# Who issues the loads of V: from SyncE in two bursts to ScalarE, one piece at a time

## The chip, the cores and the metric

The kernel runs on one core of a Trainium2 chip. The metric is the device time of one execution in microseconds; where a median is given, it is over several executions. The core's engines are named as in the profile: PE (TensorE, matrix products), ACT (ScalarE), DVE (VectorE), POOL (GpSimd) and SP (SyncE, which computes nothing and issues transfers). Each engine works through its own list of instructions in order and waits on semaphores for the others. Transfers (DMAs) can be issued by SP, ACT or POOL.

## What is computed

Causal attention with a decay bias, for 8 batches of 8 heads, 576 positions and 64 dimensions, followed by a gated feed-forward block (SwiGLU) over the 4608 tokens:

```python
scores = scale * q @ k.T
cum = cumsum(max(s, 0))
bias = -(cum[:, None] - cum[None, :])
scores = where(causal, -1e9, scores + min(bias, 0))
attn = softmax(scores)
x = (attn @ v) as [4608 tokens, 512]
g = x @ w_gate                       # 512 -> 1536
out = (g * sigmoid(g) * (x @ w_val)) @ w_out
```

## The kernel before, in words

**Units of work.** The 64 heads (batch times head) are taken in 16 groups of four; the variable `h` counts the groups, `step` the head within a group (0 to 3), and two groups make a batch. The scores of a head are made in four pieces, `ci` 0 to 3 (`score_piece`): PE multiplies K and Q into a PSUM bank (L373), ACT takes the exp into the tile `pt` (L383), POOL clears what lies above the diagonal. Later PE multiplies `pt` with V, which lies in `vt` as bf16 (L410), and DVE normalises the result into `ot` (L427). The feed-forward block works on 512 tokens at a time: PE makes gate and value products (L643), ACT a tanh (L664, tile `th`), DVE two products (L666 `pp`, L677 `ht`), and then PE the down products (L700 for the first two token tiles, L749 for the others), which ACT and DVE copy out (L717, L798, L864).

**Order.** Nothing is left to a scheduler: the generator `attn_items` yields after each small piece of attention, and a loop over the feed-forward items pumps it, so that attention of later heads runs between the feed-forward products of earlier tokens. Each engine's list has the order in which the code records the instructions. PSUM has eight banks, which both halves take and give back in turn.

**Side work.** `side(h, step, ci)` is called after each score piece and records what has to be ready later: the loads of Q and K (`load_qk`, L145), their casts to bf16 on ACT (L258), from group 5 on a way through scratch memory (`scratch`, L274, tiles `ks` and `qs`) and back by a transposing transfer (`transposes`, L284, into `pk` and `pq`), after which DVE copies them into place (`split`, L288, tile `kq`). Attention output of batches 2 and up goes to memory (L444, `xs`, issued by POOL) and comes back by a transposing transfer into `XT` (L451). All transposing transfers, the loads of Q and K, the scratch writes and, in the kernel before, the loads of V are on SP's list, in that order of recording.

**V.** `load_v(b, cs)` (L156) loads pieces of a batch's V as float32 into `rawv`; there are five pieces, 0 to 4, of 128 positions each and 64 for the last, and each piece is one transfer (L162; 256 KB, the last 128 KB, in runs of 256 bytes). `rawv` has one buffer, so the first piece of a batch waits until the batch before has been cast. `side_v` casts the pieces into `vt` (`cast_v`): for batch 2 on POOL, for batches 3 to 7 on ACT (L171), in the odd group before the batch begins. The loads of batch `bn` are recorded in group `h = 2 * bn - 2`: pieces 0 and 1 after head 2's score piece 1, and pieces 2, 3 and 4 after head 3's score piece 1. Pieces 0 and 1 thus stand between the scratch writes of a group's K and Q and the transposing transfers that fetch them, and pieces 2 to 4 behind these.

**Semaphores of transfers.** The tile framework gives each transfer of SP or ACT one of eight completion semaphores and lets it wait, before it is issued, until the transfer that last used this semaphore has landed. The wait stands in the list of the engine that issues.

Of the kernel before, what the change touches and what calls it, by code (L numbers as in the profile page):

```python
# [19 lines left out]
def kernel(  # L20
# [11 lines left out]
    nc = tc.nc  # L32
    PSUM = bass.MemoryType.PSUM

    B, H, S, D = q.shape
# [78 lines left out]
    with tc.manual_schedule():  # L114
# [37 lines left out]
        def load_qk(hb):  # L152
            load_one(hb, "k")
            load_one(hb, "q")

        def load_v(b, cs, eng=nc.sync):  # L156
            if 0 in cs:
                loaded["v", b] = raw.tile([128, NCH, H, D], FP32, tag="rawv", bufs=1, name="rawv")
            t = loaded["v", b]
            for c in cs:  # L160
                n = 128 if c < 4 else TAIL
                eng.dma_start(  # L162
                    t[0:n, c, :, :],
                    v[b, :, c * 128 : c * 128 + n, :].rearrange("h p d -> p h d"),
                )

        def cast_v(b, c, eng):
            n = 128 if c < 4 else TAIL
            dst, src_t = VT[b % 2][0:n, c, :, 0:D], loaded["v", b][0:n, c, :, :]
            if eng is nc.scalar:  # L170
                nc.scalar.copy(dst, src_t)  # L171
            else:
                eng.tensor_copy(dst, src_t)  # L173
# [9 lines left out]
        def aug(hb, engs, hhs=range(HB)):  # L183
            for hh in hhs:
                r, e = divmod(hh, 2)
                r0 = 64 * (1 - r)
                bh = hb * HB + hh
                engs[hh].dma_start(  # L188
                    KQ[hb % 2][r][r0 : r0 + 4, :, e * S : (e + 1) * S],
                    HL[bh : bh + 1, :, :, :],  # L190
                )
# [61 lines left out]
        def cast_one(hb, name, eng):  # L253
            cts[name, hb] = cp.tile([128, J, NR, D], BF16, tag="c" + name, bufs=2, name="c" + name)
            dst = cts[name, hb].rearrange("x j r d -> x r j d")
            src_t = loaded[name, hb]
            if eng is nc.scalar:
                nc.scalar.copy(dst, src_t)  # L258
            else:
                eng.tensor_copy(dst, src_t)  # L260
# [11 lines left out]
        def scratch(hb):  # L272
            for name, SC in (("k", KS), ("q", QS)):
                nc.sync.dma_start(  # L274
                    SC[hb].rearrange("(x j) c -> x (j c)", j=J),
                    cts[name, hb].rearrange("x j r d -> x (j r d)"),
                )
# [3 lines left out]
        def transposes(hb):  # L281
            for name, SC in (("k", KS), ("q", QS)):
                prs[name, hb] = cp.tile([128, NR * S], BF16, tag="p" + name, bufs=1, name="p" + name)
                nc.sync.dma_start_transpose(prs[name, hb], SC[hb])  # L284
# [186 lines left out]
        def do_later(n):  # L471
            while n > 0 and later:
                f, *args = later.pop(0)
                f(*args)
                n -= 1
# [5 lines left out]
        def side(h, step, ci):  # L481
            bh = HB * h + step
            for c in V1_AT.get((bh, ci), ()):
                cast_v(1, c, nc.gpsimd)
            if bh == H + 4 and ci == 3:
                load_v(2, range(5))
            if h == 4 and (step, ci) in ((0, 1), (2, 1)):
                load_qk(6 + step // 2)
            if h >= 5 and h + 3 < NHB and (step, ci) == (0, 1):
                load_qk(h + 3)  # L490
            hb = h + 1
            if NPE <= hb < NHB:
                late = hb == NPE
                if late and (step, ci) == (0, 1):
                    scratch(hb)
                if late and (step, ci) == (0, 3):
                    transposes(hb)
                if (step, ci) == (0, 1):
                    aug(hb, GP4)
                first = 1 if hb < NPE + 3 else 0  # L500
                if step in (first, first + 1) and ci == (3 if late else 1):
                    for r in range(NR):
                        later.append((split, hb, "kq"[step - first], r))
            hb = h + 2
            if hb == NPE and step == 3 and ci % 2 == 1:
                cast_one(hb, "kq"[ci // 2], nc.gpsimd)
            if NPE < hb < NHB:
                six = hb == NPE + 1
                if (step, ci) == ((2, 0) if six else (0, 2)):
                    cast_one(hb, "k", nc.scalar)  # L510
                if (step, ci) == ((2, 2) if six else (1, 2)):
                    cast_one(hb, "q", nc.scalar)
                if (step, ci) == ((3, 0) if six else (2, 0)):
                    scratch(hb)
                if (step, ci) == (3, 3 if six else 0):
                    do_later(NR * 2)
                    transposes(hb)
            if ci != 1:
                return
            bn = h // 2 + 1  # L520
            if 3 <= bn < B:
                if h % 2 == 0:
                    if step == 2:
                        load_v(bn, (0, 1))
                    if step == 3:
                        load_v(bn, (2, 3, 4))

        V2_AT = {(1, 0): 0, (1, 1): 1, (1, 2): 2, (1, 3): 3, (2, 0): 4}
        V_AT = {(1, 0): 0, (2, 0): 1, (2, 2): 2, (3, 0): 3, (3, 2): 4}
# [31 lines left out]
        def attn_items():  # L561
            for kk in range(H, BH + 2):
                h, step = divmod(kk, HB)
                if kk < BH:
                    if step == 0:
                        do_later(NR * 2)
                    if step == 1 and 3 < h + 1 < NPE:
                        cast_one(h + 1, "k", nc.gpsimd)
                        cast_one(h + 1, "q", nc.gpsimd)
                    if step == 2 and 3 < h + 1 < NPE:  # L570
                        aug(h + 1, GP4)
                    for ci in range(4):
                        score_piece(kk, ci)
                        side(h, step, ci)
                        side_v(h, step, ci)
                        yield kk + 0.1 + ci / 8
                        if (step, ci) in PREP_AT.get(h, ()):
                            prep_one(
                                h + 1, PREP_AT[h][step, ci],
                                (nc.scalar, nc.vector)[ci // 2] if h == 2 else None,  # L580
                            )
                            yield kk + 0.1 + ci / 8
# [327 lines left out]
        def pick(side):  # L910
            b = PICK[side]
            for lo in range(2):
                for c0, c1 in ((0, 512), (512, S)):
                    nc.tensor.matmul(
                        banks[:, b + c0 // 512, 0 : c1 - c0], sel[:, lo, :],
                        HL[:, lo, 1, c0:c1], start=(lo == 0), stop=(lo == 1),
                        skip_group_check=True,
                    )

        def picked_row(side):  # L920
            b = PICK[side]
            src_t = banks.rearrange("p b n -> p (b n)")[up, b * 512 : b * 512 + S]
            dst = KQ[0][0][up, side, 0:S]
            if side == 1:
                nc.scalar.activation(
                    dst, src_t, AF.Identity, bias=r_m[up, 0:1], scale=r_k[up, 0:1]
                )
            else:
                nc.vector.tensor_scalar(
                    dst, src_t, r_q[up, :], r_k[up, :], ALU.mult, ALU.add  # L930
                )
            give(b)
            give(b + 1)
# [102 lines left out]
        at = attn_items()  # L1036
# [84 lines left out]
```

## Time and profile before

| | |
|---|---|
| median of 3 runs | 374.61 us (373.37 to 375.18) |
| the profiled execution's own time | 373.92 us |
| its span | 372.0 us |
| busy PE / DVE / ACT / POOL | 363.2 / 291.1 / 239.9 / 212.4 us |
| V loads issued by SP | 35 (10 for batches 1 and 2, 25 for batches 3 to 7) |
| transfers from SP's queue | 41.46 MB, 46.9% of 16 DMA engines over the span |
| transfers from POOL's queue | 22.21 MB, 22.7% |

The span is what the profiler sees between the first and the last instruction; the rest of the execution's time lies around it. Busy time leaves out the issuing of transfers and the waiting. In an ACT line of the timeline the columns are start (us), duration (us), engine, source line, operation, written and read tile, shape, count, and in brackets the idle time before it and what ended it. SPq stands for SP's list of transfers.

### The profile page before, as it was taken

Reading aid. Unit: us, or ns where it says so; the run is one execution under the profiler, and the core shown is the slowest. Engines: PE = TensorE matmul, PEld = TensorE weight load, DVE = VectorE, ACT = ScalarE, POOL = GpSimd, SP = SyncE. Lnnn points to the kernel's source line nnn. Section 1 sums busy time; section 2 is a strip of 40 time slices with the busy share of each in tenths; the row PEclk is TensorE's granted clock in tenths of the full one; section 3 lists DMA queues with packets and bytes.
Section 4 is the critical chain, followed back from the end, with each engine's and each line's share of the span. In section 5 each row is a group of like instructions: output and inputs, shape, how many; then the busy total and the mean of one; then the engine's idle time right before and its main releaser. Section 6 shows DMA issues by size and latency. Waiting matters only on the chain.

```text
span 372.0 us, 8786 instructions
## 1 busy us (share of the span) xinstructions
PE 363.2 (98%) x3288; PEld 230.3 (62%) x3288; DVE 291.1 (78%) x585; ACT 239.9 (65%) x470; POOL 212.4 (57%) x325
## 2 busy tenths in 40 slices
PE   7899999999999999999999999999999999999996
PEld 6684556655555557855685558655865585476465
DVE  8978776377985899589967897699868867975984
ACT  8877776778886967688757875786565523323321
POOL 8983556955266547594749464955675516315320
PEclk9999999999999999999999999999999999999999
DMA  7999999799879996996789484994142113002003
GB/s 238 220 254 259 215 272 257 239 299 227 252 172 307 199 268 181 162 285 217 214 179 263 160 185 157 265 210 114 40 121 62 35 30 118 0 3 86 28 0 113
DMA packets 97133, 64.21 MB, mean 173 GB/s; under 512 B 77228, under 2 KB 82724, under 8 KB 97092
## 3 DMA queue, kind: packets, MB, share of 16 engines
q1 hardware_dynamic: 84964, 41.46, 46.9%
q0 software_dynamic: 12128, 22.21, 22.7%
q8 instruction: 25, 0.41, 0.5%
q14 instruction: 16, 0.13, 0.1%
HBM read 37.90 MB, written 19.86 MB: 155 GB/s over the span
## 4 chain that ended last, share of the span: by engine, by line
PE 83%; DVE 10%; DMA 2%; ACT 2%; issue 2%; POOL 1%; DVEq 0%; ACTq 0%
PE banks L643 43%; PE banks L749 17%; PE banks L373 9%; PE banks L410 7%; PE banks L700 5%; DVE kq L330 3%; DMA pk<-ks 2%; DVE pp L666 2%; DVE ht L677 1%; DVE kq L288 1%; ACT th L664 1%; POOL vt L173 1%; ACT pt L383 1%; PE banks L459 1%; PE banks L301 0%
## 5 line engine op out<-in xcount | busy, mean ns | idle before, releaser
L383 ACT ACTIVATE pt<-banks 128x512 bf16<-128x512 f32 (+1 forms) x256 | 120.4, 511 | 29.8 <-PE banks L373 17.1
L643 PE MATMUL banks<-XT,wg 128*128 128x512 bf16 x432 | 111.4, 379 | 0.4 <-DVE pp L666 0.3
L643 PE MATMUL banks<-XT,wv 128*128 128x512 bf16 x432 | 110.9, 379 | 0.1
L664 ACT ACTIVATE th<-banks 128x512 bf16<-128x512 f32 x108 | 64.7, 599 | 56.3 <-PE banks L643 51.4
L666 DVE SCALAR_TENSOR_TENSOR pp<-th,banks 128x512 bf16<-128x512 bf16 x108 | 73.7, 682 | 18.3 <-ACT th L664 18.0
L677 DVE SCALAR_TENSOR_TENSOR ht<-pp,banks 128x512 bf16<-128x512 bf16 x108 | 74.1, 687 | 10.3
L373 PE MATMUL banks<-kq 128*128 128x128 bf16 (+4 forms) x576 | 76.4, 240 | 0.8 <-DVE kq L330 0.3
L686 POOL TENSOR_TENSOR ht<-ht 128x512 bf16<-128x512 bf16 x35 | 40.4, 1154 | 53.3 <-DVE su L684 53.2
L373 PEld LDWEIGHTS <-kq 128*128 128x128 bf16 x576 | 46.1, 98 | 30.7 <-issue 2.4
L643 PEld LDWEIGHTS <-wv 128*128 128x128 bf16 x432 | 38.4, 98 | 36.2 <-issue 0.2
L643 PEld LDWEIGHTS <-wg 128*128 128x128 bf16 x432 | 38.4, 98 | 34.1 <-issue 0.7
L410 PEld LDWEIGHTS <-pt 128*128 128x128 bf16 x960 | 41.8, 98 | 17.7 <-issue 0.7
L388 POOL TENSOR_SCALAR_AFFINE_SELECT pt<-pt 128x512 bf16<-128x512 bf16 x56 | 36.6, 653 | 25.9 <-ACT pt L383 21.7
L410 PE MATMUL banks<-vt,pt 128*128 128x65 bf16 x960 | 46.8, 194 | 0.5 <-DVE ot L427 0.4
L444 POOL DMA_DIRECT2D xs<-ot x24 | 21.7, 904 | 30.4 <-DVE ot L427 28.0
L749 PEld LDWEIGHTS <-ht 128*128 128x128 bf16 x336 | 31.2, 98 | 4.3
L427 DVE TENSOR_TENSOR ot<-banks,rc 128x320 bf16<-128x320 f32 x64 | 31.5, 492 | 2.2
L188 POOL DMA_DIRECT2D kq<-HL x48 | 29.2, 610 | 0.0
L700 PE MATMUL banks<-wo,ht 128*128 128x512 bf16 x96 | 25.8, 379 | 0.0
L749 PEld LDWEIGHTS <-su 128*128 128x128 bf16 x252 | 23.6, 98 | 3.3
L814 POOL TENSOR_TENSOR ysb<-ysb 128x512 f32<-128x512 f32 x12 | 15.2, 1269 | 15.3 <-DVE ysb L808 15.3
L749 PE MATMUL banks<-WS,ht 128*128 128x256 bf16 x168 | 22.9, 273 | 0.0
(101 smaller groups left out, 377.2 us busy)
## 6 DMA issues: line engine op xcount, KB each, us to landing
out_dram<-ysb POOLq DMA_DIRECT2D x32, 256.0 KB, 4.0
rawv<-in_v_dram SPq DMA_DIRECT2D x28, 256.0 KB
rawk<-in_k_dram SPq DMA_DIRECT2D x12, 576.0 KB
rawq<-in_q_dram SPq DMA_DIRECT2D x12, 576.0 KB
xs<-ot POOLq DMA_DIRECT2D x24, 160.0 KB, 3.7
ks<-ck SPq DMA_DIRECT2D x11, 288.0 KB
qs<-cq SPq DMA_DIRECT2D x11, 288.0 KB
rawk<-in_k_dram POOLq DMA_DIRECT2D x3, 576.0 KB, 6.0
```

Source lines behind the costliest of these rows:

```text
L373: nc.tensor.matmul(sc[:, o : o + w], T[:, 1, e * S + 128 * tj : e * S + 128 * (tj + 1)], T[:, 0, e * S + lo : e * S + hi], start=not maske ...
L383: nc.scalar.activation(pt[:, c0 : c0 + n], sc, AF.Exp, scale=0.125)
L388: nc.gpsimd.affine_select(pt[:, 1088:1600], pt[:, 1088:1600], pattern=[[0, 4], [1, 128]], compare_op=ALU.is_ge, fill=zreg, base=0, channel ...
L410: nc.tensor.matmul(av[:, bi * (D + 1) : (bi + 1) * (D + 1)], pt[:, c0 : c0 + 128], VT[b % 2][:, tj, h, :], start=(tj == 0), stop=(tj == bi),)
L427: nc.vector.tensor_mul(ot[:, :, e * D : (e + 1) * D], av3[:, :, 0:D], rc[:, :, None].to_broadcast([128, NCH, D]),)
L643: nc.tensor.matmul(view(bs, TT), w[:, c, f0 : f0 + 128], xt[:, c, :], start=(c == 0), stop=(c == 3),)
L664: nc.scalar.activation(th, pg, AF.Tanh, scale=0.5)
L666: nc.vector.scalar_tensor_tensor(pp, in0=th, scalar=1.0, in1=pg, op0=ALU.add, op1=ALU.mult)
L677: nc.vector.scalar_tensor_tensor(hp[:, 2 * k2 : 2 * k2 + 2, :].rearrange("p a n -> p (a n)"), in0=pp, scalar=0.5, in1=pv, op0=ALU.mult, op ...
L686: (nc.vector if ft == NFT - 1 else nc.gpsimd).tensor_sub(hp[:, 1:3, :], hp[:, 1:4:2, :], hp[:, 0:3:2, :])
L700: nc.tensor.matmul(view(pys[ts_], DM), hps[ft // 2][:, 2 * (ft % 2) + half, c0 : c0 + 128], WO[j][:, ft % WKO, :], start=(ft == 0), stop=( ...
L749: nc.tensor.matmul(ps, lhs(p), rhs(p), start=(first and p == 0), stop=(last and p == NP - 1), skip_group_check=True,)
```

## The change

The loads of V for batches 3 to 7 are issued by ACT instead of SP, and one piece at a time, each after a score piece's exp has been recorded. For batches 4 to 7 the places are, in the same even group as before, head 1 after score pieces 1 and 3, head 2 after 1 and 3, and head 3 after 1. For batch 3 they are in groups 4 and 5: head 2 after piece 3, head 3 after 1 and 3, and head 0 of the next group after 1 and 3. Sizes, the buffer and the casts stay. Batches 1 and 2 stay as they were.

```diff
-            if ci != 1:
-                return
-            bn = h // 2 + 1
-            if 3 <= bn < B:
-                if h % 2 == 0:
-                    if step == 2:
-                        load_v(bn, (0, 1))
-                    if step == 3:
-                        load_v(bn, (2, 3, 4))
+            if h >= 4:
+                odd = h % 2
+                at = VLOAD_AT if h > 5 else V3LOAD_AT
+                if h // 2 + 1 < B and (odd, step, ci) in at:
+                    load_v(h // 2 + 1, (at[odd, step, ci],), nc.scalar)
+
+        VLOAD_AT = {(0, 1, 1): 0, (0, 1, 3): 1, (0, 2, 1): 2, (0, 2, 3): 3, (0, 3, 1): 4}
+        V3LOAD_AT = {(0, 2, 3): 0, (0, 3, 1): 1, (0, 3, 3): 2, (1, 0, 1): 3, (1, 0, 3): 4}
```

On ACT's list this adds 25 transfers, each with its semaphore wait; SP's list loses 25. The lists of PE, DVE and POOL keep their instructions and order.

## The prediction

> **What bounds the kernel now.** I read the page first for the engine that is full, then the stretches in time for where it is not full, then the chain and the waits for what made those holes.
>
> ```profile
> PE 363.2 (98%) x3288; PEld 230.3 (62%) x3288; DVE 291.1 (78%) x585; ACT 239.9 (65%) x470; POOL 212.4 (57%) x325
> ```
>
> ```profile
> 80.00:100.00 20.00, 19.75 (x184) 11.26 (x181) 17.05 (x34) 16.82 (x34) 8.87 (x16) 1.00 0.97 253
> 100.00:120.00 20.00, 20.00 (x179) 11.31 (x176) 14.74 (x30) 14.00 (x28) 12.28 (x23) 1.00 0.91 233
> 120.00:140.00 20.00, 19.60 (x168) 10.78 (x166) 17.77 (x37) 16.20 (x33) 11.05 (x17) 1.00 1.11 240
> 140.00:160.00 20.00, 20.00 (x211) 15.10 (x210) 14.82 (x33) 12.95 (x27) 12.99 (x21) 1.00 0.81 182
> ```
>
> The first fence is the page's busy time; the second has stretches of 20 us: busy PE, PEld, DVE, ACT, POOL, then the PE clock, the DMA share and GB/s. PE is the bound and its clock is full (1.00). V of batches 3 to 7 is fetched between 76 and 243 us, and there PE lacks 0.25 us (80 to 100) and 0.40 us (120 to 140), nothing else. A matmul's busy time hides short stalls, so I also look at the repeat: in the chain the down stage begins at 147.18, 186.24, 225.30 and 264.36 us, 39.06 us apart each time. A loop that repeats to 0.01 us under changing DMA traffic is paced by PE's own list. So the change can give back very little and can take much.
>
> The hole of 0.40 us is the one that V's loads touch:
>
> ```profile
> 118.37 7.22 DMA pk<-ks
> 125.62 0.84 DVE kq L288
> ```
>
> ```profile
> DVE kq L288 <- DMA pk<-ks: 1.7, 2, 1.0
> ...
> PE banks L410 <- DVE ot L427: 0.4, 1, 0.4
> ```
>
> The first fence is from the chain (start, us), the second from the waits (us, times, longest). VectorE waits for the transposed K (L288) twice, 1.0 us near 92 and 0.76 us near 125 us. Behind it on VectorE stand pp, ht and ot; PE then waits 0.4 us for ot, once. The hole near 83 us comes from a copy of pq that VectorE started 5.4 us after the data had landed, so no transfer makes it.
>
> **The change part by part.** *Taken from SP: 25 issues.* In the timeline of SP the V issues of the five batches take 7.66, 4.39, 3.84, 4.63 and 4.96 us, 25.5 us in all. SP computes nothing; what counts is what stands behind them in its order, pk and pq. Two V pieces stand between the K scratch write and pk:
>
> ```profile
> 108.94 2.45 SPq L451 DMA_TRANSPOSE XT<-xs  x2
> 111.50 0.53 SPq L274 DMA_DIRECT2D ks<-ck  x1
> 112.12 0.38 SPq L274 DMA_DIRECT2D qs<-cq  x1
> 112.55 1.81 SPq L162 DMA_DIRECT2D rawv<-in_v_dram  x2
> 118.37 2.59 SPq L284 DMA_TRANSPOSE pk<-ks  x1
> ```
>
> pk cannot be issued before ks has landed (118.3 us by the semaphore updates), so the 1.81 us of issue is hidden under that wait; but those pieces landed at 120.4 and 121.7, ahead of pk in the same queue, and pk took 7.2 us to land where the pk issued at 135.63 took 4.2. Without them I expect pk about 3 us earlier, more than VectorE's 0.76 us of waiting. Gain: 0.40 us of PE. Bounds: all of PE's idle there, 0.65 us, and -0.4 us (a loss), if V's packets from the second queue slow ks by as much as they free pk.
>
> [...]
>
> *Added to ACT: 25 issues.* No row shows ACT issuing. The nearest is SP's issue of the same piece:
>
> ```profile
> L162 SPq DMA_DIRECT2D rawv<-in_v_dram x2: 461/654/846, 151.4 to 151.9; - x2
> ```
>
> The first of a pair, behind a short queue, took 0.46 us, the second 0.85. In the new code one piece goes at a time, some 2 us apart, so I take 0.5 us; 25 x 0.5 = 12.5 us on ACT, 65% busy. The lower end is 0, because ACT's sequencer works ahead of its engine (the wait record of the exp of 88.41 begins at 86.90, while the cast of 86.42 runs), and an issue can lie beside running work; the upper end is 0.85. Against this stands ACT's idle time right behind the issues, by its timeline:
>
> ```profile
> 85.92 0.60 ACT L383 ACTIVATE pt<-banks 128x512 bf16<-128x512 f32 x1 [0.15 <-PE banks L373]
> 86.42 1.14 ACT L258 CAST ck<-rawk 128x1152 bf16<-128x1152 f32 x1
> ...
> 150.40 0.37 ACT L864 COPY s<-banks 128x256 f32<-128x256 f32 x1 [2.59 <-DVE de L866]
> ```
>
> For batch 5 (144.9 to 157.1) the gaps are 0.58, 2.59, 0.22, 0.82 and 0.75, 4.96 us for 5 x 0.5 = 2.5 us (4.25 at 0.85): hidden. Batches 6 and 7 repeat this. For batch 3 the pieces fall at about 78.7, 81.2, 82.5, 85.7 and 87.6; the first three meet gaps of 0.18, 0.15, 0.43 and 1.33, but the last two only 0.15 and 0.24, and there ACT is full (casts of K between exps). So 2 x 0.5 - 0.39 = 0.6 us of lateness reaches the exp at 88.41. The gaps up to 101 us (0.37, 0.17, 0.23, 0.73) swallow it; meanwhile pp, ht and the AV matmuls come late by up to 0.6. Cost 0 to 1.3 us (2 x 0.85 - 0.39); I take 0.4, since PE has other matmuls queued for part of it.
>
> *Added to ACT: waits.* In the built program each SP or ACT transfer takes one of eight completion semaphores, usually in turn, and is not issued before that semaphore's last transfer has landed. On SP such a wait delays transfers; on ACT it parks every exp, tanh and copy behind it. I matched each of the 25 with the landing of its predecessor in the trace. 20 or so have 1 us or more in hand; batch 3's first also waits for POOL's last cast of batch 2 (done 76.8, needed 78.7). Batch 4 is the exception. Its piece 3 waits for the XT transpose issued at 108.94, which landed at 116.31 behind 1.15 MB of K and Q; ACT gets there at about 112.3. Its piece 2 (reached at 111.0) waits for piece 0, issued at about 106.9: V pieces took 3.9 us (issued 190.06) to 7.9 us (112.55) to land, so 110.8 to 114.8. Behind piece 3:
>
> ```profile
> 112.87 0.58 ACT L717 COPY ysb<-banks 128x512 f32<-128x512 f32 x1 [0.80 <-PE banks L700]
> 114.08 0.60 ACT L383 ACTIVATE pt<-banks 128x512 bf16<-128x512 f32 x1 [0.62 <-PE banks L373]
> 114.88 0.60 ACT L383 ACTIVATE pt<-banks 128x512 bf16<-128x512 f32 x1 [0.21 <-PE banks L373]
> 115.75 0.71 ACT L383 ACTIVATE pt<-banks 128x512 bf16<-128x512 f32 x2 [0.27 <-PE banks L373]
> ...
> 117.53 0.60 ACT L664 ACTIVATE th<-banks 128x512 bf16<-128x512 f32 x1 [0.52 <-PE banks L643]
> ...
> 119.69 0.60 ACT L664 ACTIVATE th<-banks 128x512 bf16<-128x512 f32 x1 [1.07 <-PE banks L643]
> ```
>
> If XT lands at time L, the copy starts at L + 0.5 instead of 112.87; the gaps of 0.62, 0.21, 0.27, 0.52 and 1.07 (2.69) give back, piece 4 takes 0.5. At 119.69 ACT is late by L - 114.6, or 1.7 us for L = 116.3. But SP, freed of V, should bring K and Q forward: L of 113 to 115.5 costs 0 to 0.9. I take 0.4, with ends 0 and 3.7 (L 2 us later, as three V pieces now compete).
>
> In turn SP's transfers now wait on semaphores that V's pieces held; those were issued some microseconds before, and the end of -0.4 us above covers a late one. POOL and VectorE keep their order. V lands earlier than its casts need it, as before.
>
> **The sum.** -0.4 + 0.4 + 0.4 = +0.4 us. The profiled execution took 373.92 us (span 372.0 and 1.9 around it) and would become 374.3; it lay 0.7 below the median of 374.61, so I say 375.0. What a measurement here can tell from no change is about 0.5%, 1.9 us.
>
> **The rivals.**
> 1. *ACT is parked in batch 4.* Place and price as above: it decides from L of about 116.5 on; price 1.9 to 3.7, so about 377.2. For it: XT's 7.4 us to land with the DMA share at 0.91 to 1.11. Against: the transfers ahead of XT start earlier now.
> 2. *An issue costs ACT far more than 0.5 us because SP issues at the same time.* No row shows two issuers. If each waits out one SP transpose issue (median 1.18 us), it is 1.7 us, 8.4 a batch against idle of 2.75 (batch 3) and about 5 (others): 5.6 + 4 x 3.4 = 19 us of lateness, less about 3 us of idle in each following 20 us, so +4 us or more: 379. Against: in batch 5 most pieces fall where SP is idle (142 to 149 us).
> 3. *Faster by over 0.5%.* The rows offer 0.65 us of PE idle, so 374.0; only scatter (373.37 to 375.18) would carry it below 372.7.
>
> [...]
>
> **How the numbers follow.** Hidden, within 0.5%: 0.68. Rival 1: 0.17. Rival 2: 0.10. Rival 3: 0.05. So faster 0.05, same 0.68, slower 0.27. The likeliest case's own range is 373.5 to 376.4. The whole range starts at 373.4 (median less 0.65, less half a microsecond of scatter) and reaches to 378.0, over most of rival 1.
>
> **What would show it.** Right: V issues in ACT's timeline at 0.4 to 0.9 us; pk near 118 us landing in about 4 us; no wait of VectorE for pk near 125; PE at 20.00 of 20 from 140 on; the 39.06 us repeat kept. Rival 1: an ACT gap of several us near 112 that a transfer ends, and PE idle near 116 to 121. Rival 2: ACT issues of 1.2 us and more, and a longer repeat. The prediction is wrong if PE shows stalls in the repeating part, or if the casts of V wait for their data.

## The result, and the profile after

| | kernel before | changed kernel |
|---|---|---|
| median of 6 executions each | 374.26 us | 377.95 us (376.72 to 379.63) |
| ratio, 95% interval | | 1.0100 (1.0068 to 1.0131) |
| profiled execution, its span | 373.92, 372.0 us | 378.95, 377.0 us |

The changed kernel is 1.0% slower, about 3.7 us. In this document ratios leave disturbed executions out, while medians hold all of them, so a ratio need not be the quotient of two medians.

The page's busy times and the same 20 us stretches as before (columns: busy PE, PEld, DVE, ACT, POOL, then PE clock, DMA share, GB/s):

```profile
PE 364.5 (97%) x3288; PEld 231.0 (61%) x3288; DVE 291.0 (77%) x585; ACT 239.1 (63%) x470; POOL 212.3 (56%) x325
```

```profile
80.00:100.00 20.00, 19.75 (x171) 11.02 (x169) 17.73 (x36) 16.70 (x33) 8.83 (x16) 1.00 1.11 248
100.00:120.00 20.00, 17.43 (x161) 9.98 (x160) 12.70 (x25) 11.06 (x23) 8.98 (x16) 1.00 0.91 227
120.00:140.00 20.00, 20.00 (x155) 10.94 (x154) 15.79 (x33) 16.16 (x34) 11.22 (x18) 0.91 0.92 212
140.00:160.00 20.00, 20.00 (x211) 15.04 (x209) 15.93 (x35) 13.34 (x28) 12.14 (x19) 1.00 0.71 187
```

Nearly everything happens in the second and third stretch: PE is idle for 2.57 us where it was full, and then the granted clock averages 0.91. The waits (us, times, longest) name it:

```profile
ACT ysb L716 <- DMA XT<-xs: 5.7, 1, 5.7
PE banks L642 <- ACT ysb L716: 2.6, 1, 2.6
```

The copy `ysb` (L717 before, L716 now) needs nothing of `XT`. What waits for `XT` is the V issue ahead of it, as ACT's timeline shows (start, us):

```profile
110.33 1.21 ACT L383 ACTIVATE pt<-banks 128x512 bf16<-128x512 f32 x2
112.16 0.38 ACTq L162 DMA_DIRECT2D rawv<-in_v_dram  x1
112.58 0.71 ACT L383 ACTIVATE pt<-banks 128x512 bf16<-128x512 f32 x2 [1.05 <-DMA rawv<-in_v_dram]
118.46 0.38 ACTq L162 DMA_DIRECT2D rawv<-in_v_dram  x1
118.95 0.59 ACT L716 COPY ysb<-banks 128x512 f32<-128x512 f32 x1 [5.66 <-DMA XT<-xs]
```

Batch 4's piece 2 held ACT for 1.05 us (for piece 0's landing), piece 3 for 5.66 us. PE ran on with what it had until it needed the bank that the copy empties. The chain (start, us) gives the order of causes:

```profile
106.48 6.08 DMA xs<-ot
112.56 0.02 issue
112.58 5.86 DMA XT<-xs
118.44 0.02 issue
118.46 0.38 ACTq L162
118.83 0.04 issue
118.87 0.04 ACTq L716
118.91 0.04 issue
118.95 0.59 ACT ysb L716
119.55 0.04 issue
119.59 1.05 PE banks L642 x4
```

Before, the attention output `xs` left POOL at 106.04 and `XT` was issued at 108.94:

```profile
106.04 0.92 POOL L444 DMA_DIRECT2D xs<-ot  x1 [0.53 <-DVE ot L427]
```

Now `xs` took 6.08 us to land, so `XT` was issued at 112.58 and landed at 118.44 instead of 116.31. And when PE started again, it got a slower clock (stretches of 1 us, columns as above):

```profile
116.00:117.00 1.00, 1.00 (x12) 0.56 (x11) 0.34 (x1) 0.00 (x0) 0.58 (x1) 1.00 1.16 85
117.00:118.00 1.00, 0.01 (x1) 0.00 (x0) 0.68 (x2) 0.00 (x0) 0.00 (x0) 1.00 0.26 85
118.00:119.00 1.00, 0.00 (x0) 0.00 (x0) 0.00 (x0) 0.05 (x1) 0.00 (x0) 1.00 1.11 383
119.00:120.00 1.00, 0.41 (x2) 0.19 (x2) 0.00 (x0) 1.00 (x3) 0.00 (x0) 1.00 1.05 402
120.00:121.00 1.00, 1.00 (x13) 0.74 (x12) 0.00 (x0) 1.00 (x5) 0.63 (x1) 0.72 1.11 314
121.00:122.00 1.00, 1.00 (x9) 0.66 (x7) 0.00 (x0) 1.00 (x5) 0.80 (x3) 0.50 1.27 250
122.00:123.00 1.00, 1.00 (x3) 0.30 (x2) 0.82 (x3) 0.60 (x2) 0.86 (x3) 0.50 1.24 244
```

The trace's clock record has 1.0 up to 120.4 us, 0.5 for 3.4 us, then 1.0 to the last matmuls. Busy PE looks perfect in the last two lines (1.00) while it runs at half the clock: only the clock column tells.

PE has the same 3288 matmuls in the same order in both kernels, so the start of each can be set against its start before. The later the step, the more lateness has been gathered: 0.46 us at start-up (scatter, ahead of any V that moved), +2.72 at 116.4, +1.66 in the slow clock, -0.56 at 131.4, +0.72 at 248, together 5.00, against 5.03 between the two profiled executions. The -0.56 stands where the gain at `pk` was forecast. VectorE's copy of `pk`, before and after (start, us):

```profile
125.62 0.84 DVE L288 COPY kq<-pk 64x1152 bf16<-64x1152 bf16 x1 [0.76 <-DMA pk<-ks]
```

```profile
129.61 0.96 DVE L288 COPY kq<-pk 64x1152 bf16<-64x1152 bf16 x1
```

The wait is gone, but VectorE, late itself, came to this copy 5.9 us after `pk` had landed (123.67). It would not have waited for a `pk` that landed as late as before (125.59) either, so this trace does not show that moving V gave the 0.56 back. The 0.72 is in batch 7, where ACT was parked again, by its piece 3:

```profile
236.85 0.38 ACTq L162 DMA_DIRECT2D rawv<-in_v_dram  x1
237.34 0.58 ACT L797 COPY ysb<-banks 128x512 f32<-128x512 f32 x1 [2.80 <-PE banks L373]
```

The `XT` transpose that this piece's semaphore waited for landed at 236.83. The profile names a matmul as the releaser of the copy; the issue that started 0.02 us after that landing stood ahead of it. VectorE was 1.4 us later for it at first and only 0.4 us by its copy of `pk`, which then took 1.36 us instead of 0.82; how much of the 0.72 is the parking was not separated.

### The profile page after: what moved, and what is told of

Same layout as the page of the kernel before. It is cut to its first block, busy times and chain, and to the rows that moved or that the text cites. A ratio compares the mean times of both kernels' runs of the same rounds, so it can differ in the third digit from the quotient of the medians.

```text
span 377.0 us, 8792 instructions
## 1 busy us (share of the span) xinstructions
PE 364.5 (97%) x3288; PEld 231.0 (61%) x3288; DVE 291.0 (77%) x585; ACT 239.1 (63%) x470; POOL 212.3 (56%) x325
## 4 chain that ended last, share of the span: by engine, by line
PE 82%; DVE 9%; DMA 4%; ACT 2%; issue 1%; POOL 1%; DVEq 0%; ACTq 0%
PE banks L642 44%; PE banks L748 17%; PE banks L373 9%; PE banks L410 7%; PE banks L699 3%; DVE kq L330 2%; DVE pp L665 2%; DMA xs<-ot 2%; DMA XT<-xs 2%; DVE ht L676 1%; DMA kq<-HL 1%; DVE kq L288 1%; PE banks L301 1%; POOL vt L173 1%; ACT pt L383 1%
## 5 line engine op out<-in xcount | busy, mean ns | idle before, releaser
L393 POOL TENSOR_SCALAR_AFFINE_SELECT pt<-pt 128x64 bf16<-128x64 bf16 x56 | 14.7, 263 | 16.1 <-ACT pt L383 16.0
```

## The experiments

Theory A: ACT, parked in batch 4 behind the semaphore of the `XT` transpose, makes PE idle, and the idle time brings a stretch of half clock. Its rivals: issuing costs ACT in every batch (theory B), or V's packets, now earlier and from a second queue, delay other work whoever issues them.

| run | median, us | ratio to the kernel before | PE idle, 115 to 120 us | `XT` landed | from `xs` issue |
|---|---|---|---|---|---|
| changed kernel | 377.95 | 1.0100 (1.0068 to 1.0131) | 2.58, then half clock | 118.44 | 11.96 |
| batch 4 back on SP | 375.23 | 1.0007 (0.9973 to 1.0040) | 0.39 | 118.86 | 11.53 |
| batch 4 alone on ACT | 379.72 | 1.0103 (1.0063 to 1.0142) | 1.93 | 117.68 | 11.31 |
| before + 6 copies | 374.39 | 0.9998 (0.9964 to 1.0032) | 0 | 115.91 | 9.57 |
| before + 9 copies | 375.80 | 1.0039 (1.0013 to 1.0065) | 1.79 | 116.24 | 9.91 |
| before + 10 copies | 378.39 | 1.0112 (1.0056 to 1.0169) | 2.45 | 115.33 | 8.96 |
| before + 11 copies | 379.61 | 1.0127 (1.0080 to 1.0174) | 3.04, then half clock | 115.67 | 9.36 |
| batch 4: 0 to 2 on ACT | 375.32 | 1.0017 (0.9985 to 1.0049) | 0.10 | 117.26 | 11.24 |
| batch 4 on POOL, rest on ACT | 382.01 | 1.0214 (1.0155 to 1.0273) | 1.40 | 118.83 | 12.49 |
| batch 4 alone on POOL | 378.23 | 1.0083 (1.0050 to 1.0115) | 0.92 | 118.34 | 12.00 |
| batch 4 early, on SP | 375.13 | 1.0019 (0.9988 to 1.0050) | 0 | 116.59 | 10.53 |
| V behind `pk`, on SP | 375.62 | 1.0028 (0.9998 to 1.0058) | 0.05 | 116.08 | 9.27 |
| batch 4, two pieces later | 377.09 | 1.0058 (1.0023 to 1.0093) | 0.78 | 118.50 | 11.86 |

The last three columns are of the profiled execution: idle is 5 us less PE's busy time, landings are by the semaphore updates, and the last column is from POOL's issue of `xs` near 106 to the landing of `XT` (10.27 in the kernel before).

### Batch 4 back on SP

Against the changed kernel: the places of ACT hold for batches 3, 5, 6 and 7, and batch 4 falls to the lines of the kernel before.

```diff
-            if h >= 4:
+            bn = h // 2 + 1
+            if 3 <= bn < B and bn in (3, 5, 6, 7):
...
+            elif 3 <= bn < B and h % 2 == 0 and ci == 1:
+                if step == 2:
+                    load_v(bn, (0, 1))
+                if step == 3:
+                    load_v(bn, (2, 3, 4))
```

> The changed kernel, except that batch 4's V stays on SP where it was in the kernel before; batches 3, 5, 6 and 7 stay on ACT. Theory A (ACT is parked in batch 4 behind the XT transpose that owns its semaphore): no ACT gap near 112 to 119 us, PE busy for 20.0 of 20 us from 100 to 120, the granted clock 1.0 throughout; the 0.72 us of PE that batch 7 lost near 248 us may stay, and the hole of pk near 125 us comes back. So the kernel before plus 0 to 1.2 us, and 3 to 4 us below the changed kernel. Theory B (issuing transfers costs ACT, or V pieces spread in time disturb the other transfers, in every batch alike): four of the five batches still pay, so the kernel before plus 2.4 us or more.

The ratio is 1.0007: with four batches left on ACT the loss is gone, which is against theory B. The clock stayed at 1.0. The hole of `pk` that was expected back did not come: `pk` landed at 126.46, later than before, and PE, 1.85 us late by then, got 0.57 us back there all the same. The profile has a loss of another kind, in batch 3:

```profile
81.90 3.00 ACTq L162 DMA_DIRECT2D rawv<-in_v_dram  x1
82.35 0.22 ACT L383 ACTIVATE pt<-banks 128x64 bf16<-128x64 f32 x1
84.94 0.60 ACT L383 ACTIVATE pt<-banks 128x512 bf16<-128x512 f32 x1 [2.37 <-PE banks L373]
```

One issue, batch 3's piece 2, took 3.00 us instead of 0.38. SP issued nothing between 79.08 and 85.32, so it is not SP and ACT meeting. Pieces 0 and 1 had not landed (86.60 and 87.92). PE became 1.2 us later, not here but near 91 us, and the chain comes there by way of ACT's next issue, piece 3, which waited until piece 0 had landed:

```profile
77.28 9.32 DMA rawv<-in_v_dram
...
86.62 0.37 ACTq L162
```

So batch 3 can park ACT too, when its pieces land late; how the 1.2 us divide between the long issue and this wait was not separated.

### Batch 4 alone on ACT

The same kernel with the condition turned round, so that batches 3, 5, 6 and 7 stay on SP:

```diff
-            if 3 <= bn < B and bn in (3, 5, 6, 7):
+            if 3 <= bn < B and bn in (4,):
```

> The reverse: only batch 4's V is issued by ACT, one piece at a time; batches 3, 5, 6 and 7 stay on SP as before. Theory A: the ACT gap of 5 to 6 us near 113 to 119, ended by the XT transpose, is there, PE idles 2 to 3 us near 117 to 119 and then runs 3 to 4 us at half clock; the kernel before plus 3.0 to 4.5 us. Theory B: one fifth of the cost, plus 0.4 to 1.0 us.

One batch carries the whole loss: 1.0103. The waits of its profile are those of the changed kernel, somewhat shorter:

```profile
ACT ysb L722 <- DMA XT<-xs: 4.7, 1, 4.7
...
PE banks L648 <- ACT ysb L722: 1.9, 1, 1.9
```

The half clock that theory A wanted was not in this profile (376.38 us). Seven others lie in two groups, two at 375.65 and 375.85 and five from 379.23 to 380.36. The half clock can be only a part of that: the mean granted clock is 0.998 and 1.000 in the first group and 0.990 to 0.994 in three of the second, but 0.999 in the other two (379.79 and 379.93), and what made those slow no trace shows.

### ACT busy in place of waiting: 6, 9, 10 and 11 copies

Against the kernel before; the range is 6, 9 and 10 in the other three.

```diff
+            if (h, step, ci) == (6, 2, 3):
+                for _ in range(11):
+                    nc.scalar.copy(busy, busy)
```

> The kernel before, all V on SP, with 11 extra copies of a 128x512 bf16 tile onto itself on ACT at the place of batch 4's piece 3 (after head 2's score piece 3 of group 6). They add work and feed nothing. About 11 x 0.5 = 5.6 us, the length of ACT's gap in the changed kernel. Theory A, second half (ACT's absence is what matters, not the transfer; and PE's idle time of about 2.6 us brings a stretch at half the granted clock): PE idles 2 to 3 us near 117 to 120, a stretch of 3 to 4 us at half clock follows, the kernel before plus 3.5 to 4.5 us. Rival (the slow clock comes from the transfers of V in flight, or from something else in the changed kernel): PE idles as much but the clock stays 1.0, plus 2 to 3 us.

> As the run with 11 extra copies, with 6 of them (about 3 us of ACT). Theory A: ACT's gaps behind it (2.7 us up to 119.7) and the matmuls that PE has queued take most of it up: PE idles 0 to 0.6 us, no half clock, the kernel before plus 0 to 0.7 us. Rival (lateness of ACT passes through to PE in proportion): half of the other run's cost, plus 1.7 to 2.2 us.

> The kernel before with 9 extra copies at the place of batch 4's piece 3 (6 and 11 gave 3.87 and 7.12 us on ACT, PE idle of 0 and 3.04 us, and a half clock of 3.4 us only with 11). 9 copies are 5.8 us; a slope of 1 behind the first 4.1 us makes PE idle for 1.7 us. If the half clock needs an idle time longer than the 1.93 us that the run with batch 4 alone survived at full clock, the clock stays 1.0 and the time is the kernel before plus 1.4 to 1.8 us. If every idle time brings its share of slow clock, plus 2.4 us and more.

> 10 extra copies: ACT away for about 6.5 us, PE idle for about 2.4 us (9 copies gave 1.8 at full clock, 11 gave 3.04 and 3.4 us at half clock, the changed kernel 2.58 and 3.4). If the idle time that brings the half clock lies between 1.93 and 2.4 us: plus 3.5 to 4.2 us with a half clock of 3.4 us near 119; if between 2.4 and 2.58: plus 2.1 to 2.4 us at full clock; if it depends on when the idle time falls: executions of both kinds, about 1.7 us apart.

No V transfer is moved here, and the loss is there all the same: 1.0127 with 11 copies. A copy took 0.618 us, not the 0.5 expected, so ACT was away for 7.12 us and PE idle for 3.04. Six copies (3.87 us) cost nothing, nine (about 5.8) made PE idle for 1.79 us: ACT may be late by some 4 us here, and every microsecond beyond is PE's. That refutes the pass-through in proportion. The parked ACT lies close to the same line, if the hold of piece 2 is counted in: 5.66 + 1.05 us of absence and 2.58 us of idle time in the changed kernel, 4.72 + 1.34 and 1.93 with batch 4 alone on ACT. On the clock, with 11, 10 and 9 copies (stretches of 1 us):

```profile
118.00:119.00 1.00, 0.00 (x0) 0.00 (x0) 0.00 (x0) 0.94 (x3) 0.00 (x0) 1.00 1.31 277
119.00:120.00 1.00, 0.12 (x1) 0.10 (x1) 0.00 (x0) 1.00 (x3) 0.00 (x0) 0.72 0.91 188
120.00:121.00 1.00, 1.00 (x3) 0.30 (x2) 0.00 (x0) 1.00 (x3) 0.60 (x1) 0.50 1.08 93
```

```profile
118.00:119.00 1.00, 0.00 (x0) 0.00 (x0) 0.00 (x0) 0.97 (x3) 0.00 (x0) 1.00 0.92 172
119.00:120.00 1.00, 0.70 (x4) 0.34 (x4) 0.00 (x0) 1.00 (x3) 0.18 (x1) 1.00 1.02 230
120.00:121.00 1.00, 1.00 (x17) 0.73 (x16) 0.00 (x0) 1.00 (x4) 0.55 (x2) 1.00 1.29 282
```

```profile
118.00:119.00 1.00, 0.40 (x2) 0.19 (x2) 0.00 (x0) 1.00 (x4) 0.00 (x0) 1.00 0.95 149
119.00:120.00 1.00, 1.00 (x17) 0.73 (x16) 0.00 (x0) 1.00 (x4) 0.63 (x1) 1.00 0.93 196
```

With 10 copies the profiled execution (376.27 us) idled 2.45 us and paid nothing more. Of the three others two have a mean granted clock of 0.995 (377.83 and 380.68 us) and one of 0.999 (378.96). So there are executions of both kinds, the third of the outcomes set down, but their times do not fall 1.7 us apart as it had them. What the kind hangs on was not shown.

### Only pieces 0 to 2 of batch 4 on ACT

Against the kernel before, whose lines the other batches keep:

```diff
+            if bn == 4:
+                if (h % 2, step, ci) in VLOAD_AT and VLOAD_AT[h % 2, step, ci] < 3:
+                    load_v(bn, (VLOAD_AT[h % 2, step, ci],), nc.scalar)
+                if h % 2 == 0 and (step, ci) == (3, 1):
+                    load_v(bn, (3, 4))
```

> Only batch 4 is changed: its pieces 0 to 2 are issued by ACT at the changed kernel's places, its pieces 3 and 4 by SP where they were before; the other batches stay on SP. Theory A says that piece 3's wait for the XT transpose is the one that costs: without it ACT may wait 1 to 2 us for piece 0 ahead of piece 2, which its gaps take up; PE idles 0 to 0.5 us from 110 to 125, clock 1.0 throughout, the kernel before plus 0 to 0.7 us. Rival (the traffic of pieces 0 to 2 beside K, Q and the xs write makes the later work late whoever waits): ACT or PE are late by some other wait, plus 1.5 us or more.

1.0017: without pieces 3 and 4 no loss can be told. It is their wait, not the first three issues, that costs.

### The same traffic from POOL

Against the changed kernel; the second run has only this group's loads on POOL and all other batches on SP, as before.

```diff
-                load_v(h // 2 + 1, (at[odd, step, ci],), nc.scalar)
+                load_v(h // 2 + 1, (at[odd, step, ci],), nc.gpsimd if h == 6 else nc.scalar)
```

> The changed kernel with batch 4's five pieces issued by POOL at the same places; batches 3, 5, 6 and 7 stay on ACT. The pieces are in flight at about the same times, but the semaphore wait, if any, stands in POOL's list. Theory A: no ACT gap that a transfer ends from 110 to 120 us, PE idles 0 to 0.5 us there; as the run with batch 4 on SP, so the kernel before plus 0 to 1.2 us. Rival (V's packets at this time are the cause): PE idles 2 us or more near 117 to 119 whatever engine issues, plus 2.5 us or more.

> Only batch 4's five pieces are issued by POOL at the changed kernel's places; all other batches stay on SP. The run with batch 4 on POOL and the others on ACT had XT land at 118.83 us, PE idle 1.4 us for it at 117, and a second loss of 2.5 us near 217, where one DVE sum took 2.66 us beside POOL. If that second loss and the slow executions there were chance or came from the other batches: the kernel before plus 0.8 to 1.8 us, clock 1.0. If V from POOL itself brings them: plus 4 us or more, with PE idle near 217 again.

Theory A alone falls here. ACT was not parked, and still PE idled, now for `XT` itself, as the chain of the run with batch 4 alone on POOL shows:

```profile
106.34 5.44 DMA xs<-ot
111.79 0.02 issue
111.80 6.54 DMA XT<-xs
118.34 0.04 issue
118.39 0.38 PE banks L647
```

PE needs `XT` at about 117.5 us. With `XT` at 118.34 it idled 0.92 us, with 118.83 it idled 1.40. So an `XT` as late as the changed kernel's (118.44) costs PE about 1 us whoever issues V, and ACT's parking made 2.58 of it.

Both runs cost more than that, because of a second loss near 217, far from batch 4 and in both profiles alike: VectorE becomes 2.43 us later there, and PE idles 1.9 us. In the run with batch 4 alone on POOL, the `xs` issue there began at 216.03 (214.06 before), masks and a product followed on POOL without a pause up to 219.47, and a DVE sum (L689) that started at 216.96 took 2.66 us; in the kernel before it took 0.28. The same in two different programs, it is hardly chance. Why five more POOL transfers put that `xs` off was not tried.

### Batch 4 early, but on SP

Against the kernel before:

```diff
+            if h == 6 and (step, ci) in ((1, 1), (1, 3), (2, 1)):
+                load_v(4, ({(1, 1): 0, (1, 3): 1, (2, 1): 2}[step, ci],))
...
+                        load_v(bn, (2, 3, 4) if bn != 4 else (3, 4))
```

> Nothing on ACT: batch 4's pieces 0 and 1 are issued by SP right behind the loads of K and Q (near 108 to 109 us), ahead of the XT transpose, and piece 2 right behind the scratch writes; the rest as before. So V's early packets are there without any engine of the computation waiting for a semaphore. Combined theory (the early pieces make xs and XT late by 1 to 2 us, and parking ACT adds to that): XT lands at 117.3 to 118.8 instead of 116.3, and PE, which needs it at about 117.3, idles 0 to 1.5 us with the clock at 1.0; the kernel before plus 0 to 1.2 us. Theory A alone (parking is everything): plus 0, whenever XT lands.

`XT` landed at 116.59, earlier than either theory said, although pieces 0 and 1 went out at 106.27 and 106.78 and `XT` could be issued only 6.5 us after `xs`. PE was full:

```profile
115.00:120.00 5.00, 5.00 (x44) 2.83 (x44) 3.32 (x7) 3.14 (x7) 4.39 (x8) 1.00 0.69 184
```

So in this trace early packets of V alone did not make `XT` late. Down the table's last column, the seven programs with all V on SP need 8.96 to 10.53 us from `xs` to `XT`, the six with pieces of batch 4 on ACT or POOL 11.24 to 12.49. On SP a piece stands in order with the transpose; from a second issuer it goes out beside it (in the changed kernel piece 2 at 112.16, `XT` at 112.58). That this is the reason is argued, not shown: here piece 2 went out at 116.76, 4 us behind `XT`, so the issuer and the time of piece 2 changed together. The run with batch 4 back on SP, at 11.53, is outside this split, and nothing tried explains it.

`pk` landed at 124.95 here, 0.64 us earlier than before, and VectorE is 0.5 to 0.7 us earlier from 126 us on, without ACT. But with 6 copies, V untouched, it landed at 124.22, and PE got 0.34 us back. One trace of each does not tell a gain at `pk` from the scatter of its landing.

### All V behind pk, on SP

Against the kernel before:

```diff
-                    if step == 2:
-                        load_v(bn, (0, 1))
-                    if step == 3:
-                        load_v(bn, (2, 3, 4))
+                if h % 2 == 0 and step == 3:
+                    load_v(bn, range(5))
```

> The kernel before, with all five V pieces of batches 3 to 7 issued by SP behind pk and pq, at the place where pieces 2 to 4 stood. If the changed kernel's one gain (pk near 125 us lands without two V pieces ahead of it, 0.56 us of PE) doesn't need ACT, this kernel has it without parking any engine that computes: VectorE's wait for pk near 125 us is gone, the kernel before minus 0.3 to 0.6 us, which is within what a measurement can tell from no change. Rival (V so late that its casts wait for it in the odd groups): plus 1 us or more, with ACT waiting for rawv near 130 us.

The rival's wait is there: `pk` was on time (landed at 120.33), but now V is what is late. The kernel before does not have this wait:

```profile
ACT vt L171 <- DMA rawv<-in_v_dram: 2.0, 2, 1.1
```

VectorE became 0.6 us later there, and PE was idle for 0.73 of the 20 us from 120 on, against 0.40 before. The ratio of 1.0028 (0.9998 to 1.0058) lies at the rival's price of 1 us but does not clear no change.

### All on ACT, batch 4's last two pieces later

Against the changed kernel:

```diff
-                at = VLOAD_AT if h > 5 else V3LOAD_AT
+                at = V3LOAD_AT if h <= 5 else V4LOAD_AT if h == 6 else VLOAD_AT
...
+        V4LOAD_AT = {(0, 1, 1): 0, (0, 1, 3): 1, (0, 2, 1): 2, (0, 3, 1): 3, (0, 3, 3): 4}
```

> The changed kernel, all 25 pieces on ACT, with batch 4's pieces 3 and 4 recorded two score pieces later (after head 3's pieces 1 and 3 instead of head 2's 3 and head 3's 1). Piece 3 has the same semaphore and still waits for the same XT transpose, but the copy of the PSUM bank (ysb) that PE waited for and three exps now stand ahead of it on ACT. Combined theory (XT is late by 1 to 2 us because V comes from a second queue, and PE has to wait for it whoever issues; the rest is ACT being away): XT lands at 117.5 to 118.8, PE idles 0.3 to 1.5 us and waits for XT itself, clock 1.0; with 0.6 gained at pk and up to 0.7 lost in batch 7 the kernel before plus 0.3 to 1.8 us, 2 us or more below the changed kernel. If the time of V's packets alone were the cause: as the changed kernel, plus 3.5 us.

`XT` landed at 118.50 and PE waited for it, as expected, and the clock stayed at 1.0 in the profile. But the ratio of 1.0058 is above the range given and only about 0.4% below the changed kernel's. The profile tells why: the park moved to piece 1,

```profile
111.85 0.38 ACTq L162 DMA_DIRECT2D rawv<-in_v_dram  x1
112.27 0.59 ACT L717 COPY ysb<-banks 128x512 f32<-128x512 f32 x1 [2.94 <-PE banks L373]
```

whose semaphore belonged to the `XT` transpose before, which landed at 111.83. `pk` took 7.8 us, and VectorE waited 0.68 us for it, and batch 3's piece 2 took 2.81 us to issue. A place on ACT's list chosen after one trace does not hold in the next.

No version that moves V beat the kernel before. Three cannot be told from it: batch 4 back on SP (1.0007), its pieces 0 to 2 on ACT (1.0017) and batch 4 early on SP (1.0019).

## Why the prediction was wrong

Hidden, within 0.5%, was the likeliest case, and rival 1 came true: its place (piece 3 at ACT, behind the `XT` transpose), its mechanism and about its price (377.2 against 377.95; the range went to 378.0). The price is near partly by luck: it took too much for ACT's lateness and nothing for the clock. The step that failed is the third term of the sum, "Added to ACT: waits", +0.4 us for L of 113 to 115.5; in the profiled execution it was 4.4 us, with L at 118.44.

- *L.* Measured: 118.44, above even the case set at its upper end. The reason given, that SP freed of V brings K and Q forward, was half true: K was issued at 106.52 instead of 107.81. But `XT` does not follow K and Q alone; it waits for `xs`, POOL's transfer, which I left out. `xs` met V's piece 0 (106.62), K and Q in flight and took 6.08 us. K and Q alone can make most of that: with 9 and 10 copies, where Q went out at 105.97 and 105.79 and no V was in flight, `xs` took 5.63 and 5.26 us. But there `XT` landed at 116.24 and 115.33 all the same; in the changed kernel V's piece 1 (landed at 115.90) and piece 2, issued beside `XT`, were in flight too. Which of them held `XT` was not separated. The working counted V's second queue as a load on `XT` at its upper end alone.
- *From lateness to PE.* I summed ACT's gaps up to 119.69, which for L = 118.4 gives 3.8 us of lateness on ACT; PE's idle time was 2.6 to 2.7. The copies show the form here: nothing up to about 4 us of absence, then one for one.
- *The clock.* Nothing in the sum had PE itself slower after an idle time: 1.66 us of the 4.4 lost at batch 4 in the profile.
- *The gain at pk*, -0.40: not shown. `pk` was issued at 120.31 and took 3.4 us instead of 7.2; it landed at 123.67, 1.9 us earlier than before, not 3. VectorE's wait is gone and PE got 0.56 us back, but with 11 copies, V untouched, PE got 0.57 us back at the same place, and 0.57 with batch 4 back on SP: whoever comes late finds `pk` there.
- *Batches 5 to 7 hidden:* right for 5 and 6 (VectorE's instructions stand 4.27 us later at 164, 190, 205 and 229 us, so the repeat is kept), wrong for 7, where up to 0.72 us was lost, through the same kind of wait at least in part: by the old landings its pieces had time in hand, in the new trace three of its transfers landed just before the issue they held (233.38, 236.83 and 239.00).

*Issue time*, +0.4 with ends 0 and 1.3, was over-sized for the changed kernel. The group of V loads by ACT (min/median/max in ns, first and last start):

```profile
L162 ACTq DMA_DIRECT2D rawv<-in_v_dram x25: 374/383/688, 77.6 to 239.0; - x25
```

An issue can also lie inside running work (108.66, during the cast of 107.91 to 109.05). No lateness of PE was added between 9 and 116 us, so batch 3 cost nothing in this trace. Rival 2 asked for 1.2 us and more wherever SP issues too; at 82.27 ACT issued during SP's `pk` issue (81.98 to 83.36) in 0.38 us, the median of all 25, so at this meeting no wait shows. Rival 2's size did occur, 3.00 and 2.81 us for batch 3's piece 2 in two other traces, but with SP silent. The upper end of 0.85 us was read from batch 5 alone: in the kernel before, SP's second piece of batch 3 (at 77.29) took 3.13 us to issue.

## What to carry to other kernels

A transfer that is given to a computing engine brings its semaphore's wait along (5.66 us for piece 3), and that wait is for some other transfer's landing. Before moving it, find whose landing that is, follow that transfer back to what releases it (here `xs` of a third engine), and assume the landing comes later than in the old trace (here 118.44 us instead of 116.31, with the moved pieces 1 and 2 in flight). A price for a stall on a full PE can have two parts, the idle time and the clock after it (here 2.58 and 1.66 us); and a wait that is gone is a gain only if the engine that waited did not come later for another reason.

## What the runs showed of the hardware

**A slow clock came with some idle times of PE and not with others.** In the changed kernel the granted clock was 0.5 for 3.4 us from 120.4 us on, 0.9 us after the end of 2.58 us of idle time; with 11 copies it was 0.5 for 3.4 us as well, from about 119.4 on, in an idle time of 3.04 us. It stayed at 1.0 in the profiles with 10 copies (2.45 us of idle time), with batch 4 alone on ACT (1.93) and with 9 copies (1.79), and in the kernel before it was 1.0 for 365.2 us without a break. Half of 3.4 us is 1.7 us of work; the changed kernel's matmuls became 1.66 us later in that stretch.

Executions of one kernel differ in it. The mean granted clock is 0.991 to 0.995 in four of the changed kernel's six, in three of four with 11 copies, in two of four with 10 and in none of ten with 9; in the others it is 0.998 or more. Single executions of the kernel before have a low one too (0.994 at 376.81 us). The clock does not make all of the spread, as batch 4 alone on ACT shows. What decides whether an idle time brings the slow clock was not shown.

**An issue on ACT is cheap until it is not.** It took 0.38 us (median of 25) beside running work, but 2.81 and 3.00 us for one piece in two of the four traces with batch 3 on ACT; in the kernel before, SP's longest for V of batches 3 to 7 is 3.13 us, so it is not ACT's alone. Both times on ACT the two pieces ahead landed late (86.19 and 87.16, 86.60 and 87.92, against 83.82 and 85.91 where the issue took 0.38); what held the issue was not separated.

**DVE and POOL.** A DVE sum of 0.28 us took 2.66 us when it began while POOL worked without a pause, in two runs. No run took POOL's work away to test it.
